# Sink attention and a feed-forward layer on one core: later splits moved one step up, one step's values pulled ahead, the last pair's products reordered

## The chip, the core and the metric

The kernel runs on one core of a Trainium2 chip, as one program without collectives. The metric is the time of one execution in device microseconds, taken as the median over runs. The parts of the core are called by the profile's names: PE (matmul) with PEld (its weight loads), ACT, DVE, POOL, and SP, which issues the DMAs.

## The reference, cut to what matters

```python
def _attn_ref(q, k, v, n_sink, window):            # (4, 8, 768, 64) each, n_sink 4, window 128
    scores = np.matmul(q, k.transpose(0, 1, 3, 2)) / np.sqrt(D)
    keep = is_sink | in_window                      # first n_sink keys, and 0 <= row - col < window
    scores = np.where(keep, scores, -1000000000.0)
    a = np.exp(scores - np.max(scores, axis=-1, keepdims=True))
    a = a / (np.sum(a, axis=-1, keepdims=True) + 1e-09)
    return np.matmul(a, v)

def _moe_ref(x, w_in, w_out):                       # x (3072, 512), w_in (512, 2048), w_out (2048, 512)
    h = x @ w_in
    sp = np.maximum(h, 0.0) + np.log1p(np.exp(-np.abs(h)))
    return (h * erf(sp)) @ w_out
```

The attention's result, with its eight heads side by side, is the x of the feed-forward layer.

## The kernel before

**Tiling.** The 3072 rows are twelve groups of 256 (`NG`), three to a batch. A group is four attention steps (`NPAIR`), one for each pair of heads, and then a feed-forward part. Step s belongs to group s // 4, so step 11 is the last of group 2, step 12 the first of group 3 and step 15 the last of group 3. All loops are unrolled in Python.

**An attention step.** `prep` transposes q and k (tile `tqk`, line 298) and ACT copies them (`kq`, line 301). `score` multiplies (line 349) into the single buffer `ps`. DVE masks (362) and finds the row's minimum (367). ACT takes the exponent (371); `mark["e", s]` names the last one. `norm` divides by the sums on DVE (378 to 386) and forms the sink part `snk` (390); `mark["s", s]` names it. `ptrans` transposes the weights on PE (`tp`, line 402, then `ts`, line 403; `mark["p", s]` is the last of `tp`), ACT copies them to `pa` and `pz` (409 to 415), POOL cuts them to the window (420). `av` multiplies by the values (457), and `xfin` splits the result into `xh` (ACT, 475) and `xl` (DVE, 476). `tqk`, `tp`, `ts` and `av` share two PSUM buffers.

**The feed-forward part.** For each of sixteen columns f of a group `hidden` multiplies (line 655, four chunks c of x, three products each) into one of two `h` buffers, two columns to a buffer. `act` runs on the pair: ACT lines 668 to 673, DVE 677, then `gh` (DVE 684) and `gl` (POOL 685). Its first product (677, out `u`, in `u` and `h`) is the last reader of the `h` buffer. `project` adds up both 128-row halves i of the group in two `o` tiles, three products each for every f (lines 700 to 702, the third with `gl`). `result` copies each `o` tile to `ot` (706), and line 617 writes it out. The tiles `u` of line 673 and `ot` share four buffers (`UB`).

**The splits.** Up to the middle of group 1 the weights are used as plain fp32. From then on each weight block is used as a rounded part and a rest: `wsplit` makes the first with an ACT cast (570) and the second with a DVE subtraction (571), in new tiles of the pool `wo` of 33 buffers. The eight splits n = 16 to 23, the first half of `w_out`, are due at m = 31 to 35 and have a mark of their own, `LATE`.

**What sets the order.** Each piece of work gets a priority key from the stage `a` in which it is written and a constant of its kind (`at`, `O`). A list scheduler then orders each engine's queue, taking in its own model of time the ready instruction of the smallest key. A split has a large key and is otherwise ready early, so it goes into the first free place. `follow(prev, ins)` adds an order without a semaphore: `ins` stands behind `prev` in the same engine's queue. Queues run in order on the chip.

**Step 11's exception.** In `core(s)`, from group 2 on, the values of step s - 2 are multiplied just ahead of the scores of step s, and the scores follow them. Step 11 alone is an exception: its `av` and `xfin` are written one and two stages behind the scores of step 12, and the scores of step 13 stand behind step 12's `tp` transposes instead.

Of the kernel before, what the change touches and what calls it, by code (L numbers as in the profile page):

```python
# [19 lines left out]
P = 128  # L20
# [19 lines left out]
NE, AL = 4, 2  # L40
# [3 lines left out]
LATE = 31  # L44

FH = 8

PW, EA = 256, 12
O = dict(prep=-100, norm=-100, core=-300, av=-300, load=-400, dup=-100, kcopy=-50, ptrans=-200, xfin=-100,
# [7 lines left out]
def kernel(  # L57
# [11 lines left out]
    nc = tc.nc  # L69
    B, H, S, D = q.shape  # L70
    NT, DM = out.shape
    DF = w_in.shape[1]
    NPAIR = H // 2
    NC = DM // P
    NF = DF // P
    GT = 256
    GPB = S // GT
    NG = B * GPB
# [56 lines left out]
    def fast_path():  # L135
        with ExitStack() as st:
# [145 lines left out]
            def follow(prev, ins):  # L282

                if prev is not None:
                    tc.add_manual_dep(
                        ins.ins, prev.ins.name,
                        mybir.DependencyInfo(mybir.DependencyClass.NoSync, mybir.DependencyReason.DATA), reason="order",
                    )
                return ins
# [15 lines left out]

            def core(s):

                prev = mark["p", s - 1] if s - AL == 3 * NPAIR - 1 else None
                late = s - AL >= 2 * NPAIR and s - AL != 3 * NPAIR - 1
                if late:  # L310
                    prev = av(s - AL)
                if s < NSTEP:
                    score(s, prev)
# [174 lines left out]
            for s in range(NSTEP + AL):  # L488
# [15 lines left out]
                if s < 2 * NPAIR:  # L504
                    x = pos(s) + (3 if s < NE else 5)
                    plan.setdefault(x, []).append(("av", av, s))
                    plan.setdefault(x + 1, []).append(("xfin", xfin, s))
                elif s == 3 * NPAIR - 1:
                    plan.setdefault(pos(s + 1) + 1, []).append(("av", av, s))
                    plan.setdefault(pos(s + 1) + 2, []).append(("xfin", xfin, s))  # L510
                if s - AL >= 2 * NPAIR and s - AL != 3 * NPAIR - 1:
                    plan.setdefault(pos(s) + 1, []).append(("xfin", xfin, s - AL))
            STAGES = ("xfin", "norm", "ptrans", "av", "kcopy", "prep", "core", "dup", "load")

# [48 lines left out]
            def wsplit(n, m):  # L563

                t = wf[n]
                d = wt[n] = wpool.tile([P, 2, DM], F32R, tag="wo", name=f"wt_{n}")
                x, y = mlp.mark[min((m - 1) // 2, NF) - 1]
                if m >= LATE:
                    x, y = mark["e", 3 * NPAIR], mark["s", 3 * NPAIR]
                follow(x, nc.scalar.copy(d[:, 0, :], t))  # L570
                follow(y, nc.vector.tensor_tensor(d[:, 1, :], t, d[:, 0, :].bitcast(F32), op=ALU.subtract))

# [24 lines left out]
            for m in range(-LEAD, NG * NF + LAG + 2):  # L597
# [11 lines left out]
                if 0 <= w < NG * NF:  # L609
                    g2, f2 = divmod(w, NF)  # L610
                    with at(a, "proj"):
                        mlp.project(gs[w // 2], g2, f2, lambda ins: follow(ahead if live and f and g >= 2 else None, ins))
                    if f2 == NF - 1:
                        for i in range(2):
                            r0 = (g2 * 2 + i) * P
                            with at(a, "res"):
                                nc.sync.dma_start(out[r0 : r0 + P, :], mlp.result(g2, i))
                if live:
                    if f == 0:
                        with at(a, "hid"):  # L620
# [17 lines left out]
    class make_mlp:  # L638
# [46 lines left out]
            nc.gpsimd.tensor_tensor(gl, acc, gh.bitcast(F32), op=ALU.subtract)  # L685
            return gh, gl

        def project(self, gt, g, f, behind=lambda ins: ins):
            if f == 0:
                for i in range(2):  # L690
                    self.acc[g, i] = self.ps_o.tile([P, DM], F32, tag="o", name=f"o_{g}_{i}")
            for i in range(2):
                o = self.acc[g, i]
                n0 = (f % 2) * GT + i * P
                ws = slice(n0, n0 + P)
# [5 lines left out]
                nc.tensor.matmul(o, gh[:, ws], wt[16 + f][:, 1, :], start=False, stop=False)  # L701
                nc.tensor.matmul(o, gl[:, ws], wt[16 + f][:, 0, :], start=False, stop=(f == NF - 1))  # L702

        def result(self, g, i):
            ot = self.work.tile([P, DM], F32, tag="u", bufs=UB, name=f"ot_{g}_{i}")
            nc.scalar.copy(ot, self.acc.pop((g, i)))  # L706
            return ot

    def general_path():
# [145 lines left out]
```

## Time and profile before

| what | value |
|---|---|
| time, median of 3 runs | 736.34 us (736.04 to 736.58) |
| the profiled execution | 736.62 us |
| its span, first to last instruction | 734.7 us |
| PE busy | 714.6 us, 97% |
| ACT busy | 552.2 us, 75% |
| DVE busy | 490.0 us, 67% |
| POOL busy | 215.8 us, 29% |
| granted TensorE clock, mean | 0.998 |

The profile is one execution. Its span leaves out 1.92 us of the 736.62 us that lie around the first and the last instruction. Times in its rows count from the first instruction. A row of the timeline gives start, length, engine, line, operation and tiles, the count where equal neighbours were merged, and in brackets the idle time of the engine just before it and what ended that. Matmuls are pipelined: the ends of two neighbours overlap, so distances are read from start to start.

### The profile page before, as it was taken

The page shows a single profiled execution, that of the slowest core. Times are in us where ns is not written, and L with a number is a line of the kernel's source. Part 1 is how long each engine was busy: PE and PEld are TensorE (multiplying, and loading weights), DVE is VectorE, ACT ScalarE, POOL GpSimd, SP SyncE. Part 2 cuts the span into 40 slices and gives each one's busy share as a digit, 9 for nine tenths or more (in the row PEclk, how much of TensorE's full clock was granted, in tenths as well). Part 3 has the DMA queues.
Part 4 walks back from the last instruction along what each step waited for, and adds up shares of the span by engine and source line. Part 5 has one row for each costly group of instructions (what it writes and reads, how often), then busy time and mean ns, then how long its engine had stood idle before and what let it go on. Part 6 is the DMA issues. An engine that isn't in the chain of part 4 may idle for free. (4 is left out here: it accounts for less than half of the span.)

```text
span 734.7 us, 16449 instructions
## 1 busy us (share of the span) xinstructions
PE 714.6 (97%) x5824; PEld 598.5 (81%) x5824; DVE 490.0 (67%) x1371; ACT 552.2 (75%) x1313; POOL 215.8 (29%) x306
## 2 busy tenths in 40 slices
PE   6889999999999999999999999999999999999997
PEld 3666667687888888888888888888888888898885
DVE  7999997877665765665665665665665666575352
ACT  5687759969887876976976885985986886776572
POOL 3411432042323322422323342233234223223221
PEclk9999999999999999999999999999999999999999
DMA  7999011113122121212222212311311321200000
GB/s 182 276 355 376 13 37 55 24 44 88 45 53 73 46 53 45 61 43 57 67 48 51 73 38 46 82 37 43 78 45 37 81 58 34 71 10 3 29 1 33
DMA packets 113001, 53.07 MB, mean 72 GB/s; under 512 B 91728, under 2 KB 105552, under 8 KB 112912
## 3 DMA queue, kind: packets, MB, share of 16 engines
q1 hardware_dynamic: 112352, 51.87, 26.2%
q8 instruction: 49, 0.80, 0.5%
q14 instruction: 40, 0.33, 0.1%
q10 hardware_dynamic: 560, 0.07, 0.1%
HBM read 38.01 MB, written 6.29 MB: 60 GB/s over the span
## 5 line engine op out<-in xcount | busy, mean ns | idle before, releaser
L655 PE MATMUL h<-xh,wt 128*128 128x256 f32 x1408 | 276.2, 284 | 0.7 <-DVE u L677 0.6
L655 PEld LDWEIGHTS h<-xh,wt 128*128 128x128 f32 x1408 | 223.8, 188 | 7.7 <-issue 1.8
L685 POOL TENSOR_TENSOR g<-u,g 128x512 fp32r<-128x512 f32 x84 | 111.2, 1324 | 366.4 <-DVE g L684 361.2
L655 PE MATMUL h<-xl,wt 128*128 128x256 f32 x704 | 197.9, 282 | 0.0
L673 ACT ACTIVATE u<-r 128x512 f32<-128x512 f32 x288 | 161.6, 622 | 14.9 <-DVE gf L677 4.9
L677 DVE SCALAR_TENSOR_TENSOR u<-u,u 128x512 f32<-128x512 f32 x168 | 131.9, 785 | 18.5 <-ACT u L673 4.0
L655 PEld LDWEIGHTS h<-xl,wt 128*128 128x128 f32 x704 | 132.1, 188 | 4.6 <-issue 0.7
L701 PE MATMUL o<-wt,g 128*128 128x512 f32 x336 | 133.9, 399 | 0.0
L700 PE MATMUL o<-wt,g 128*128 128x512 f32 x336 | 133.9, 398 | 0.0
L702 PE MATMUL o<-wt,g 128*128 128x512 f32 x336 | 130.0, 398 | 0.2 <-POOLq L823 0.2
L677 DVE SCALAR_TENSOR_TENSOR u<-u,h 128x512 f32<-128x512 f32 x84 | 57.6, 686 | 84.6 <-ACT u L673 82.5
L371 ACT ACTIVATE pst<-pst,neg 128x144 f32<-128x144 f32 x192 | 77.5, 406 | 26.6 <-DVE neg L367 25.7
L420 POOL TENSOR_SCALAR_AFFINE_SELECT pz<-pa 64x256 f32<-64x256 f32 (+1 forms) x96 | 54.2, 564 | 117.6 <-ACT pa L409 114.3
L700 PEld LDWEIGHTS o<-wt,g 128*128 128x128 f32 x336 | 63.0, 188 | 11.9 <-ACT ot L706 0.4
L702 PEld LDWEIGHTS o<-wt,g 128*128 128x128 f32 x336 | 61.9, 188 | 13.3 <-POOLq L823 0.7
L701 PEld LDWEIGHTS o<-wt,g 128*128 128x128 f32 x336 | 63.0, 188 | 11.3 <-issue 0.3
L668 ACT ACTIVATE r<-h 128x512 f32<-128x512 f32 x96 | 56.6, 589 | 17.8 <-PE h L655 14.3
L684 DVE CAST g<-u 128x512 fp32r<-128x512 f32 x84 | 36.6, 436 | 47.1 <-PE o L702 43.9
L670 ACT ACTIVATE r<-r 128x512 f32<-128x512 f32 x96 | 60.6, 632 | 2.5
L669 ACT ACTIVATE r<-r 128x512 f32<-128x512 f32 x96 | 60.7, 632 | 2.4
L301 ACT COPY kq<-tqk 128x512 f32<-128x512 f32 x48 | 27.8, 580 | 32.1 <-PE tqk L298 28.7
L349 PE MATMUL ps<-kq 64*64 64x208 f32 (+2 forms) x768 | 48.2, 361 | 0.6 <-ACT kq L304 0.5
(88 smaller groups left out, 923.1 us busy)
## 6 DMA issues: line engine op xcount, KB each, us to landing
ws<-in_moe_w_in_dram SPq DMA_DIRECT2D x16, 512.0 KB, 6.4
ws<-in_moe_w_out_dram SPq DMA_DIRECT2D x16, 512.0 KB, 8.3
out_dram<-ot SPq DMA_DIRECT2D x24, 256.0 KB, 2.2
v<-in_v_dram SPq DMA_DIRECT2D x56, 96.0 KB, 2.3
q<-in_q_dram SPq DMA_DIRECT2D x80, 64.0 KB, 2.1
k<-in_k_dram SPq DMA_DIRECT2D x80, 64.0 KB, 2.1
vz<-v SPq DMA_DIRECT2D x80, 64.0 KB, 2.0
kq<-kq SPq DMA_DIRECT2D x28, 64.0 KB, 2.1
```

The lines of the kernel that those rows point to most:

```text
L371: mark["e", s] = nc.scalar.activation(y, y, AF.Exp, bias=d["neg"][:, i, h : h + 1], scale=-1.0, accum_out=d["sum"][:, i, h : h + 1])
L420: nc.gpsimd.affine_select(out=out, in_=x, pattern=[[0, 2], [0, 2 - i0], [-sg, HP]], compare_op=op, fill=0.0, base=0, channel_multiplier=sg,)
L655: last = nc.tensor.matmul(o, wt[NC * j + c][:, p, fs], xt[e][:, c, :], start=(m == 0), stop=(m == len(ops) - 1))
L668: nc.scalar.activation(r, h, AF.Tanh, bias=b_t, scale=0.5)
L669: nc.scalar.activation(r, r, AF.Square, bias=b_v, scale=-0.5)
L670: nc.scalar.activation(r, r, AF.Square, bias=b_r)
L673: sq = nc.scalar.activation(u, r, AF.Square, bias=b_a[i], scale=CS)
L677: pr = nc.vector.scalar_tensor_tensor(out=acc, in0=u, scalar=CC[i] * CS**2, in1=x, op0=ALU.add, op1=ALU.mult)
L685: nc.gpsimd.tensor_tensor(gl, acc, gh.bitcast(F32), op=ALU.subtract)
L700: behind(nc.tensor.matmul(o, gh[:, ws], wt[16 + f][:, 0, :], start=(f == 0), stop=False))
L701: nc.tensor.matmul(o, gh[:, ws], wt[16 + f][:, 1, :], start=False, stop=False)
L702: nc.tensor.matmul(o, gl[:, ws], wt[16 + f][:, 0, :], start=False, stop=(f == NF - 1))
```

## The change

It has three parts.

- The exception of step 11 holds for steps 11 and 15. The values of step 15, until now multiplied ahead of the scores of step 17, are multiplied one stage behind the scores of step 16, and its `xfin` a stage later. The scores of step 17 stand behind step 16's `tp` transposes.
- The eight late splits stand behind step 11's last exponent on ACT and its `snk` on DVE, where they stood behind those of step 12.
- For the last two columns f of the last group, the six products of the first output tile are written ahead of the six of the second, where the order was column by column. The second tile's copy from PSUM is divided: ACT takes the left 256 columns and DVE the right 256.

```diff
+EARLY = (11, 15)
@@ core
-                prev = mark["p", s - 1] if s - AL == 3 * NPAIR - 1 else None
-                late = s - AL >= 2 * NPAIR and s - AL != 3 * NPAIR - 1
+                prev = mark["p", s - 1] if s - AL in EARLY else None
+                late = s - AL >= 2 * NPAIR and s - AL not in EARLY
@@ plan
-                elif s == 3 * NPAIR - 1:
+                elif s in EARLY:
                     plan.setdefault(pos(s + 1) + 1, []).append(("av", av, s))
                     plan.setdefault(pos(s + 1) + 2, []).append(("xfin", xfin, s))
-                if s - AL >= 2 * NPAIR and s - AL != 3 * NPAIR - 1:
+                if s - AL >= 2 * NPAIR and s - AL not in EARLY:
                     plan.setdefault(pos(s) + 1, []).append(("xfin", xfin, s - AL))
@@ wsplit
                 if m >= LATE:
-                    x, y = mark["e", 3 * NPAIR], mark["s", 3 * NPAIR]
+                    x, y = mark["e", 3 * NPAIR - 1], mark["s", 3 * NPAIR - 1]
@@ the loop over m
-                        mlp.project(gs[w // 2], g2, f2, lambda ins: follow(ahead if live and f and g >= 2 else None, ins))
+                        behind = lambda ins: follow(ahead if live and f and g >= 2 else None, ins)
+                        if w < NG * NF - 2:
+                            mlp.project(gs[w // 2], g2, f2, behind)
+                        elif f2 == NF - 1:
+                            for i in range(2):
+                                for e in range(2):
+                                    mlp.project(gs[w // 2], g2, f2 - 1 + e, behind, (i,))
@@
-                                nc.sync.dma_start(out[r0 : r0 + P, :], mlp.result(g2, i))
+                                nc.sync.dma_start(out[r0 : r0 + P, :], mlp.result(g2, i, NG - 1))
@@ project
-            for i in range(2):
+            for i in rows:
@@ result
-            nc.scalar.copy(ot, self.acc.pop((g, i)))
+            acc = self.acc.pop((g, i))
+            if g == last and i == 1:
+                nc.scalar.copy(ot[:, : DM // 2], acc[:, : DM // 2])
+                nc.vector.tensor_copy(ot[:, DM // 2 :], acc[:, DM // 2 :])
+            else:
+                nc.scalar.copy(ot, acc)
```

## Rows read from the trace of the kernel before

**Rows 1.** The page: busy time by engine, and PE's busy tenths in 40 slices.
```profile
PE 714.6 (97%) x5824; PEld 598.5 (81%) x5824; DVE 490.0 (67%) x1371; ACT 552.2 (75%) x1313; POOL 215.8 (29%) x306
...
PE   6889999999999999999999999999999999999997
```

**Rows 2.** Stretches of 10 us: length, busy PE, PEld, DVE, ACT, POOL, clock, DMA share, GB/s.
```profile
170.00:180.00 10.00, 9.41 (x67) 7.25 (x65) 8.79 (x23) 9.94 (x27) 2.45 (x5) 1.00 0.23 51
180.00:190.00 10.00, 9.69 (x89) 7.98 (x89) 6.05 (x21) 7.38 (x16) 3.26 (x7) 1.00 0.39 109
190.00:200.00 10.00, 9.68 (x78) 8.41 (x79) 7.00 (x15) 9.65 (x26) 4.28 (x6) 1.00 0.10 26
200.00:210.00 10.00, 10.00 (x87) 8.81 (x84) 7.59 (x25) 8.17 (x21) 1.49 (x2) 1.00 0.27 61
```

**Rows 3.** Timeline of PE: the work just behind its four waits.
```profile
176.59 0.39 PE L655 MATMUL h<-xh,wt 128*128 128x256 f32 x1 [0.59 <-DVE u L677]
...
179.76 0.40 PE L701 MATMUL o<-wt,g 128*128 128x512 f32 x1
180.29 0.50 PE L402 MATMUL tp<-ident,pst 128*128 128x128 f32 x2
...
186.38 0.44 PE L298 MATMUL tqk<-ident,k 128*128 128x128 f32 x2 [0.17 <-DMA v<-in_v_dram]
...
194.18 0.69 PE L402 MATMUL tp<-ident,pst 128*128 128x128 f32 x3 [0.32 <-ACT r L670]
```

**Rows 4.** Timeline of ACT and DVE: the late splits and what follows them.
```profile
166.91 2.69 ACT L570 CAST wt<-wf 128x512 fp32r<-128x512 f32 x5
...
174.06 1.67 ACT L673 ACTIVATE u<-r 128x512 f32<-128x512 f32 x3
...
168.45 4.30 DVE L571 TENSOR_TENSOR wt<-wf,wt 128x512 fp32r<-128x512 f32 x7
...
174.21 0.69 DVE L571 TENSOR_TENSOR wt<-wf,wt 128x512 fp32r<-128x512 f32 x1
...
175.85 0.69 DVE L677 SCALAR_TENSOR_TENSOR u<-u,h 128x512 f32<-128x512 f32 x1
```

**Rows 5.** Timeline of ACT, DVE and PE between step 11's and step 12's marks.
```profile
159.29 0.59 ACT L409 COPY pa<-tp 128x512 f32<-128x512 f32 x1 [1.37 <-PE tp L402]
...
162.59 0.37 ACT L475 CAST xh<-av 128x256 fp32r<-128x256 f32 x1 [2.07 <-PE av L457]
...
164.46 0.41 ACT L371 ACTIVATE pst<-pst,neg 128x144 f32<-128x144 f32 x1 [1.50 <-DVE neg L367]
...
162.99 0.43 DVE L476 TENSOR_TENSOR xl<-av,xh 128x256 fp32r<-128x256 f32 x1 [2.21 <-ACT xh L475]
...
165.26 0.42 DVE L476 TENSOR_TENSOR xl<-av,xh 128x256 fp32r<-128x256 f32 x1
...
165.75 0.37 PE L655 MATMUL h<-xl,wt 128*128 128x256 f32 x1
```

**Rows 6.** Timeline of SP and ACT: group 1's results on their way out.
```profile
180.89 1.06 SPq L617 DMA_DIRECT2D out_dram<-ot x2
...
185.06 0.64 ACT L673 ACTIVATE u<-r 128x512 f32<-128x512 f32 x1 [2.22 <-DMA out_dram<-ot]
185.60 0.73 ACT L413 COPY pz<-ts 64x256 f32<-64x256 f32 x2
```

**Rows 7.** Timeline of PE: step 13's scores, then step 17's behind step 15's values.
```profile
172.01 0.46 PE L349 MATMUL ps<-kq 64*64 64x144 f32 x2
172.40 0.33 PE L403 MATMUL ts<-ident,snk 128*128 128x128 f32 x1
172.66 0.85 PE L349 MATMUL ps<-kq 64*64 64x144 f32 x14
173.44 0.50 PE L701 MATMUL o<-wt,g 128*128 128x512 f32 x1
...
225.96 0.99 PE L349 MATMUL ps<-kq 64*64 64x208 f32 x16
226.88 0.44 PE L298 MATMUL tqk<-ident,k 128*128 128x128 f32 x2
```

**Rows 8.** The end: pieces of the last chain, and the output DMAs of the last stretch.
```profile
729.46 0.24 PE o L702
729.70 0.02 issue
729.73 0.58 ACT ot L706
...
DMA to landing us min/median/max: 2.2/2.5/2.7
```

More of the change, by code (lines that the diff above doesn't have):

```diff
@@ L686, in act, with project @@
             return gh, gl
-        def project(self, gt, g, f, behind=lambda ins: ins):
+        def project(self, gt, g, f, behind=lambda ins: ins, rows=(0, 1)):
             if f == 0:
@@ L702, in project, with result @@
                 nc.tensor.matmul(o, gl[:, ws], wt[16 + f][:, 0, :], start=False, stop=(f == NF - 1))
-        def result(self, g, i):
+        def result(self, g, i, last=None):
             ot = self.work.tile([P, DM], F32, tag="u", bufs=UB, name=f"ot_{g}_{i}")
-            nc.scalar.copy(ot, self.acc.pop((g, i)))
+            acc = self.acc.pop((g, i))
[4 more added lines that the diff above has]
+                nc.scalar.copy(ot, acc)
             return ot
```

## The prediction

> **What bounds the kernel now.** The page comes first: PE is busy 97% of the span, and its tenths read 9 or more from the fourth slice to the last but one [rows 1]. Work on the other engines therefore counts only where PE waits for it. Next I read the stretches of 10 us: behind 60 us PE falls short of full in few of them, and in the region that this change touches in three, from 170 to 200 us, while the next one is full again [rows 2]. The reader is to see there that ACT (9.94) and DVE (8.79) are nearly full in the first of these. Then the timeline of PE tells the four waits [rows 3]. They are 0.59 us in front of the hidden products at 176.59; a step from 179.76 to 180.29, 0.53 us where products of this kind follow each other at 0.23 (the pitch of the last chain's 0.24 in [rows 8]); 0.17 at 186.38 and 0.32 at 194.18. The idle column gives 0.59 + 0.17 + 0.32 and I add 0.30 for the second: about 1.4 us in all. That is the most that the first two parts can win by taking waits away. The third part is read from the last chain and the output's landing.
>
> **The splits: what they cost now.** The scheduler puts them as early as their mark lets it: five casts stand on ACT from 166.91, seven subtractions without a gap on DVE from 168.45, the eighth at 174.21 [rows 4]. They fall in front of the activation of the pair whose `h` buffer PE needs next. Line 673 starts at 174.06, and the first product on DVE, which frees the buffer, at 175.85; it ends at 176.54 and PE goes on at 176.59 [rows 3, 4]. So the first wait is the splits' doing. The second is the chain of step 13: its masks and minima stand behind the eighth subtraction, and its transposes come late. The third and the fourth are not theirs alone: ACT stands 2.22 us until an output DMA has landed, and the copies of `ts` that PE waits for (they end at 186.33) stand behind it in ACT's queue [rows 6]; the row's own releaser, a load, had long been done. The fourth is the normalising of step 14, whose DVE work queued behind the same stall.
>
> **The splits: where they go.** The work stays the same, eight casts and eight subtractions; no DMA and no PE instruction is moved with them. A cast takes 2.69 / 5 = 0.54 us and a subtraction 4.30 / 7 = 0.61 us [rows 4], so 4.3 us on ACT and 4.9 us on DVE. Behind step 11's marks ACT has idle times of 1.37 + 2.07 + 1.50 = 4.94 us and DVE of 2.21 us before step 12's softmax [rows 5]. ACT can hide all eight; DVE hides three or four, and the others come behind step 12's `snk` at the latest, where they used to be, but half of them and done some 2 us sooner. That is enough for the activation to be in time (its product at about 173 where PE needs it at 176). Queued behind a split are, on ACT, the copies of step 11's `tp` and the `xh` casts, on DVE the `xl` of steps 10 and 11. An instruction already running isn't cut short, so each idle time can overrun by one split. PE's hidden products at 165.75 start right behind the `xl` that ends at 165.68 [rows 5]: no slack there. I price this overrun between 0 and 0.6 us and take 0.2, since the idle times are wide against one split. Of the 1.4 us of waits I book all as won in the forecast: with the early backlog gone step 13's chain is ready sooner than PE, and `ts` is then transposed ahead of the stalled ACT instruction. Bounds: 0 (first rival) to 1.4.
>
> **Step 15's values.** Nothing is added; the value products, one cast and one subtraction move up some 10 us. A gain is excluded, because PE is full from 200 us on, at 9 or more tenths in every slice up to the end [rows 1, 2], and has no wait there that they could end. The cost is an extra change of PE's form of work. Step 13, which has this order now, shows it: its scores are cut by `ts` and take 172.01 to 173.44, 1.43 us, where step 17's take 225.96 to 226.88, 0.92 us, behind the values [rows 7]. The difference of 0.5 us holds about 0.1 us for `ts`, which is paid anyway. So 0 (scores that follow other work cleanly) to 0.5 us; I take 0.3. No load is late for it: the values' buffer comes free earlier, and SP's loads behind it with it. What becomes late next is nothing before step 17's own exponent, which gets more time.
>
> **The last pair.** All twelve products remain, and the third of a tile still waits for `gl`; while it waits, the second tile's two first products can fill in, as now. PE's end stays at 729.70. The first tile is complete some four products earlier than the second (4 x 0.24 = 0.9 us, now 0.7), so its copy and DMA leave about 0.25 us sooner. The second tile's copy now takes 0.58 us [rows 8]. Its halves: ACT's cast of 256 columns out of PSUM takes 0.37 us, DVE's subtraction with such an input 0.42 [rows 5], an upper bound for a plain copy. Side by side they take 0.42 us, 0.16 less; one behind the other 0.37 + 0.42 + 0.04 = 0.83, 0.25 more. The trace has no two engines reading one PSUM tile at once. The nearest rows, `xh` and `xl` of one `av` tile, run one after the other: 162.59 + 0.37 = 162.96, then 162.99 [rows 5], though there the second needs the first. I take the series. In return the two output DMAs are issued 1.1 us apart instead of 0.64. The last two landed after 2.2 and 2.7 us [rows 8]; if the second does as the first, 0 to 0.6 us come back, and I take 0.35. Sum of this part: 0.25 - 0.35 = -0.1, bounds +0.25 and -0.8. DVE's own closing instructions move behind its copy, under two microseconds of landing.
>
> The Trainium skill, "PSUM — Partial Sum Buffer", section "PSUM bank collisions raise a hardware error", says that two engines must not touch one bank and quadrant at the same time, reads against reads included, so that accesses have to be guarded by bank. The tile is one bank there; by that rule the halves go in series, the sum's choice, and the side-by-side case falls away. No run here shows such a collision.
>
> **The sum.** -1.4 + 0.2 + 0.3 - 0.1 = -1.0 us on the profiled execution: 736.62 - 1.0 = 735.6. The median of the runs is 0.28 below the profiled one, so 735.3.
>
> **Rivals.**
> 1. *The output DMA holds the gate.* Its issue at 180.89 follows a full SP queue of loads that this change doesn't move, and its landing at 185.05 doesn't care how early ACT is [rows 6]. If ACT's order stays, PE comes earlier to 186.38 and waits there for longer: the 0.59 and 0.30 won before are given back, and 0.17 and 0.32 stay. Then 0 + 0.2 + 0.3 - 0.1 = +0.4, with the overrun hidden behind the same gate +0.1 to +0.2: 736.7 profiled, 736.4 as median. For it: the wait is absolute in time. Against: it needs `ts` to stay behind line 673 in ACT's queue, and step 13's earlier chain speaks against that.
> 2. *More is won.* All waits go, the cut through step 13's scores goes too (0.4), step 15 costs nothing, the output comes 0.4 to 0.8 sooner: -1.4 - 0.4 - 0.5 = -2.3, 734.0 as median.
> 3. *Slower: the splits stand in front of step 11's `xl`.* If all eight subtractions are queued before 165.26, DVE needs 4.9 us where 2.21 us are free, and PE's products at 165.75 come 2.7 us late [rows 4, 5]. The later waits, which hang on ACT and DVE as well, aren't won back: +2.7 + 0.3 - 0.1 = +2.9, 739.2 as median. It decides from six subtractions ahead of that `xl` on (6 x 0.61 - 2.21 = 1.45 us).
> 4. *The splits don't move*, because no buffer of `wo` is free at step 11. The casts at 166.91 ran without a gap, so buffers were free then; whether earlier the rows don't show. +0.3 - 0.1: 736.5.
>
> **How the numbers follow.** What a measurement can tell from no change is 0.2%, 1.47 us: faster means below 734.87, slower above 737.81. Forecast 735.3, its own range 734.6 to 736.0: chance 0.45, of which 0.13 lies below 734.87. Rival 1: 0.25, same. Rival 2: 0.16, faster. Rival 3: 0.11, of which 0.10 is slower. Rival 4: 0.03, same. Faster 0.13 + 0.16 = 0.29; slower 0.10 and 0.02 for rival 1 with a long overrun, 0.12; same 0.59. The range leaves out half of rival 2 and nearly all of rival 3: 734.1 to 737.2.
>
> **What would show it.** Right: eight casts among ACT's idle times between 157 and 167, no more than four subtractions behind step 12's `snk`, no wait of PE at the product that frees the `h` buffer, PE full from 170 to 200. Wrong: an idle time of PE at the `xl` of step 11; ACT still standing for the output DMA and PE behind it; the scores of step 17 uncut at their old length; the two halves of the last copy overlapping, or the output landing no sooner.

## The result and the profile after

| kernel | median | range | ratio to before, 95% |
|---|---|---|---|
| before | 736.34 us | 736.04 to 737.9, 5 runs | |
| changed | 740.3 us | 740.01 to 740.98, 5 runs | 1.0053 (1.0041 to 1.0064) |

The change makes the kernel slower, by 4.0 us. The profiled execution took 740.3 us, its span 737.6 us, so 2.7 us lie outside the span, where the kernel before had 1.92. The page of after has PE as busy as [rows 1] and POOL busier, 223.5 us where it was 215.8, though POOL's work is the same:

```profile
PE 714.7 (97%) x5824; PEld 598.4 (81%) x5824; DVE 491.0 (67%) x1372; ACT 551.7 (75%) x1313; POOL 223.5 (30%) x306
```

The stretches of 10 us (columns as in [rows 2]) show where PE lost and won:

```profile
160.00:170.00 10.00, 8.01 (x105) 6.42 (x104) 8.81 (x22) 6.56 (x19) 7.90 (x8) 1.00 0.16 36
170.00:180.00 10.00, 10.00 (x84) 8.84 (x83) 5.68 (x22) 8.93 (x25) 2.59 (x5) 1.00 0.29 65
180.00:190.00 10.00, 10.00 (x94) 8.59 (x94) 3.86 (x11) 7.23 (x16) 2.71 (x5) 1.00 0.36 102
190.00:200.00 10.00, 10.00 (x64) 8.68 (x64) 7.75 (x26) 8.90 (x24) 1.63 (x3) 1.00 0.22 48
...
280.00:290.00 10.00, 9.27 (x94) 7.72 (x93) 5.48 (x28) 5.65 (x22) 3.89 (x6) 1.00 0.24 54
```

The three stretches from 170 to 200 us are full: the four waits of [rows 3] are gone, as forecast. In their place PE stands 2 us at 161 to 163 us, where it had been full, and again near 283 us. The timeline of PE names these places, and between them step 17's scores:

```profile
160.86 0.40 PE L708 MATMUL o<-wt,g 128*128 128x512 f32 x1
163.25 0.73 PE L709 MATMUL o<-wt,g 128*128 128x512 f32 x2 [1.99 <-POOL g L692]
...
228.51 0.56 PE L350 MATMUL ps<-kq 64*64 64x208 f32 x2
229.01 0.33 PE L404 MATMUL ts<-ident,snk 128*128 128x128 f32 x1
229.26 0.98 PE L350 MATMUL ps<-kq 64*64 64x208 f32 x14
230.18 0.38 PE L662 MATMUL h<-xl,wt 128*128 128x256 f32 x1
...
283.29 0.89 PE L403 MATMUL tp<-ident,pst 128*128 128x128 f32 x4 [0.25 <-DVE pst L387]
284.08 0.30 PE L404 MATMUL ts<-ident,snk 128*128 128x128 f32 x1
284.86 0.67 PE L458 MATMUL av<-pa,v 128*64 128x64 f32 x12 [0.47 <-ACT pa L410]
```

The first wait is the dearest, and its releaser is POOL. The product that stands is the third of the three (line 702 before, 709 after), the one with `gl`. The timeline of ACT, DVE and POOL tells why `gl` is late:

```profile
156.50 2.69 ACT L571 CAST wt<-wf 128x512 fp32r<-128x512 f32 x5
...
158.38 3.69 DVE L572 TENSOR_TENSOR wt<-wf,wt 128x512 fp32r<-128x512 f32 x6
...
158.54 4.65 POOL L692 TENSOR_TENSOR g<-u,g 128x512 fp32r<-128x512 f32 x1 [6.68 <-DVE g L691]
...
281.30 1.29 POOL L692 TENSOR_TENSOR g<-u,g 128x512 fp32r<-128x512 f32 x1 [0.36 <-DVE g L691]
...
281.91 0.70 DVE L379 TENSOR_SCALAR sum<-sum 128x4 f32<-128x4 f32 x1 [0.69 <-ACT pst L372]
```

Six late subtractions run on DVE from 158.38 to 162.07. POOL's one subtraction, 1.29 us at its usual length, starts at 158.54 and takes 4.65 us; it ends 1.12 us behind the last of the six. In the kernel before seven of the eight ran in a row at 168.45 [rows 4], when POOL had nothing to do. At 281.91 it is the other way round: a DVE operation on four columns takes 0.70 us, where its like took 0.17 at 156.63, and ends with POOL's subtraction at 282.6.

Last the end. The kernel ends with `tc.If(ok == 0)`, a second, general path that these executions jump over: each engine's program closes with a branch and, behind the jump, a semaphore instruction. The two halves of the last copy run in series, and these closing instructions follow (the view of the branch's line: count, duration in ns, start):

```profile
732.16 0.37 ACT L715 COPY ot<-o 128x256 f32<-128x256 f32 x1 [0.29 <-PE o L709]
...
732.56 0.42 DVE L716 COPY ot<-o 128x256 f32<-128x256 f32 x1 [4.06 <-ACT ot L715]
```
```profile
L835 DVEq COMPARE_BRANCH  x1: 72/72/72, 733.5 to 733.5; - x1
...
L835 ACTq EVENT_SEMAPHORE  x1: 17/17/17, 735.3 to 735.3; - x1
L835 DVEq EVENT_SEMAPHORE  x1: 21/21/21, 736.5 to 736.5; - x1
```

The same view of the kernel before, whose line is 823:

```profile
L823 DVEq COMPARE_BRANCH  x1: 72/72/72, 726.3 to 726.3; - x1
...
L823 DVEq EVENT_SEMAPHORE  x1: 21/21/21, 729.2 to 729.2; - x1
```

DVE needs 3 us from its branch to its next instruction. Before, these ran under the last products; after, they start only behind DVE's copy and end at 736.5, over a microsecond behind the output's landing at 735.2. Not every engine needs that long: POOL's step from the branch on takes 0.8 us (729.2 to 730.0).

**The balance of the two profiled executions.** From the first hidden product of group 1 (96.99 before, 97.94 after) to the last product PE took 632.70 and 634.18 us: +1.5. From the last product to the end of the execution: 5.0 + 1.94 and 5.44 + 2.74: +1.2. The first hidden product itself came 0.95 us later; up to there the programs are the same, and it lies between 96.6 and 99.3 us in all the runs below, so I don't count that part as the change's. By the medians it is 4.0 all the same, and by those of the runs below 2.6 for the first two parts and 1.2 for the third; where the traces' 2.7 and the medians' 4.0 part is not settled. Part of it may be the execution shown of the kernel before: three runs below that leave its middle as it is (`last`, `order`, `touch`) need 632.05 to 632.49 us for PE's stretch.

### The profile page after: what moved, and what is told of

Its sections match the earlier page's. It is cut to its first block, busy times and chain, and to the rows that moved or that the text cites. A ratio compares the mean times of both kernels' runs of the same rounds, so it can differ in the third digit from the quotient of the medians.

```text
span 737.6 us, 16453 instructions
## 1 busy us (share of the span) xinstructions
PE 714.7 (97%) x5824; PEld 598.4 (81%) x5824; DVE 491.0 (67%) x1372; ACT 551.7 (75%) x1313; POOL 223.5 (30%) x306
## 5 line engine op out<-in xcount | busy, mean ns | idle before, releaser
L692 POOL TENSOR_TENSOR g<-u,g 128x512 fp32r<-128x512 f32 x84 | 114.9, 1368 | 360.0 <-DVE g L691 343.5
L421 POOL TENSOR_SCALAR_AFFINE_SELECT pz<-pa 64x256 f32<-64x256 f32 (+1 forms) x96 | 57.2, 596 | 120.5 <-ACT pa L410 117.2
```

The lines of the kernel that those rows point to most:

```text
L421: nc.gpsimd.affine_select(out=out, in_=x, pattern=[[0, 2], [0, 2 - i0], [-sg, HP]], compare_op=op, fill=0.0, base=0, channel_multiplier=sg,)
```

## The experiments

Five theories are named in the expectations. **A**: VectorE's row of subtractions holds up GpSimd's, and TensorE waits for that. **B**: the prediction's own account. **C**: the end costs because VectorE's closing instructions come behind its share of the copy. **D**: the waits further down come from how much of TensorE's work stands in its queue between a step's last score product and its first transposition (the cover of the softmax), and behind `tp`, until the next product needs one of the two PSUM buffers that `tqk`, `tp`, `ts` and `av` share. The cover is counted in the queue's order by the pitches of the rows, 0.118 us for `h`, 0.233 for `o`, 0.109 for `tqk`; step 16 has 21 + 21 + 4 products before, 7.8 us. **E**: step 15's cost is an output transfer stuck behind loads.

| run | what differs from before | ratio, 95% |
|---|---|---|
| splits | the splits behind step 11 | 1.0027 (1.0015 to 1.0039) |
| step15 | step 15's values | 1.0024 (1.0014 to 1.0034) |
| step15b | the same again | 1.0028 (1.0017 to 1.0039) |
| last | the third part | 1.0019 (1.0009 to 1.0028) |
| order | the third part without the divided copy | 1.0003 (0.9994 to 1.0013) |
| touch | 16 columns of the last copy on DVE | 1.0020 (1.0010 to 1.0029) |
| splits15 | parts one and two | 1.0035 (1.0022 to 1.0048) |
| casts | only the eight casts behind step 11 | 1.0061 (1.0039 to 1.0082) |
| sq15_pr15 | the splits behind pair 15's own instructions | 1.0050 (1.0033 to 1.0067) |
| first19 | the first three splits behind step 11 | 0.9981 (0.9971 to 0.9990) |
| first19b | the same again | 0.9976 (0.9967 to 0.9986) |
| first20 | the first four | 1.0028 (1.0018 to 1.0038) |
| fill16 | first19, nine products moved | 0.9999 (0.9989 to 1.0010) |
| step15_pool | step15, two outputs issued by POOL | 1.0013 (1.0004 to 1.0022) |

**Each part alone.** `splits` and `step15` have one of these two edits each; `last` has the whole third part of the change's diff, `order` the same without its last hunk and the argument that goes with it (the copy stays whole on ACT).

```diff
@@ splits
-                    x, y = mark["e", 3 * NPAIR], mark["s", 3 * NPAIR]
+                    x, y = mark["e", 3 * NPAIR - 1], mark["s", 3 * NPAIR - 1]
@@ step15, and the same two tests in the plan
-                prev = mark["p", s - 1] if s - AL == 3 * NPAIR - 1 else None
-                late = s - AL >= 2 * NPAIR and s - AL != 3 * NPAIR - 1
+                prev = mark["p", s - 1] if s - AL in (11, 15) else None
+                late = s - AL >= 2 * NPAIR and s - AL not in (11, 15)
```

> The kernel before with the late splits' mark moved to step 11 and nothing else. Theory A, from the changed kernel's trace: six subtractions in a row on DVE keep POOL from its own two-input subtraction, which takes 4 to 5 us instead of 1.3, and PE waits about 2 us for that rest near 161 us; the four waits of before between 170 and 200 us (1.4 us) are mostly gone. So +0.3 to +1.2 us, with that one wait of about 2 us in the trace. Theory B, from the prediction: the splits hide, the 1.4 us are won and the loss comes from the other parts: -0.8 to -1.4 us and no wait of PE near 161 us.

> The kernel before with step 15's values ahead and nothing else. The prediction's term: +0.3 us (0 to 0.5), as an extra change of PE's form of work, with step 17's scores cut by a transpose. Rival: the reordering that it sets off further on costs more, as two waits of together 1 us in front of a transpose and of values near 282 us in the changed kernel: +1.0 to +1.6 us. If these two waits belong to the splits instead, none of them is seen here.

> The kernel before with the last pair's order and the divided copy, and nothing else. The prediction's term: -0.1 us (+0.25 to -0.8). Theory C, from the changed kernel's trace: the copy's halves run in series, the output lands no later, but DVE now passes the branch at the program's end 3 us after the last copy and the closing barrier waits for it: +0.4 us inside the span and +0.8 us behind it, +1.2 us in all.

> The kernel before with the last pair's products first tile then second, and ACT copying both tiles whole. Theory C: DVE has no work behind the products, so the end keeps its length or wins from the first tile's earlier output: -0.1 to -0.5 us. If the order of the products itself costs, as a longer wait for the last rest, +0.4 us or more.

All three parts cost: 738.55 us, 738.42 us and 738.01 us, beside 736.78 of before. The order of the last products alone costs nothing, 736.72. So the divided copy is what costs at the end, 1.2 to 1.3 us, and theory B falls for every part. Where the end's cost shows was expected otherwise: in `last` the span behind the last product grows by 2.0 us (7.03 for 5.00) and what lies outside it shrinks by 0.5 (1.39 for 1.94), while in the changed kernel both grow; only the sums agree, and how they divide isn't explained. The two waits of the whole change near 283 us are in neither `splits` nor `step15`: they belong to both parts together. In the run of the splits PE (timeline) waits at the same product as in the whole change, and twice more at step 16:

```profile
162.20 0.73 PE L702 MATMUL o<-wt,g 128*128 128x512 f32 x2 [1.99 <-POOL g L685]
...
225.21 0.89 PE L402 MATMUL tp<-ident,pst 128*128 128x128 f32 x4 [0.66 <-DVE pst L386]
...
226.77 0.55 PE L457 MATMUL av<-pa,v 128*64 128x128 f32 x8 [0.47 <-ACT pa L409]
```

At 207 us, counted by the pitches of the products done since 140 us, this run stands within 0.2 us of the kernel before: the 2 us at 162 are paid for by before's four waits and the loss around them. What stays is step 16: another 1.8 us, so that the run costs more than the 0.3 to 1.2 us expected.

**The end: 16 columns.**

```diff
-            nc.scalar.copy(ot, self.acc.pop((g, i)))
+            acc = self.acc.pop((g, i))
+            if g == last and i == 1:
+                nc.scalar.copy(ot[:, : DM - 16], acc[:, : DM - 16])
+                nc.vector.tensor_copy(ot[:, DM - 16 :], acc[:, DM - 16 :])
+            else:
+                nc.scalar.copy(ot, acc)
```

> The kernel before with one edit: of the very last tile's copy, ScalarE moves 496 columns and VectorE the other 16; the order of the last products and everything else stay. Theory C (VectorE's program ends with a branch and a fetch of instructions that took it 3 us in the kernel before under the last products, and in the changed kernel came behind its copy): the two engines' parts take about as long in series as ScalarE's whole copy did (0.58 us there, so 0.6 to 0.9 here), but VectorE's last instructions again come 3 us behind its copy, and the time rises by 1.0 to 1.4 us, to 1.0014 to 1.0019 of before, with the span's end about 7.0 us behind the last product instead of 5.0, or the difference outside the span. Rival (the cost of the divided copy lies in the copy and in the transfer behind it): the copy ends at most 0.3 us later, and the time is 0 to 0.3 us over before, 1.0000 to 1.0004.

It was 737.8 beside 736.38, so +1.4 us, with the copy only 0.19 us longer (0.81 behind the last product, before 0.62) and the landing no later (3.20 behind it, before 3.39). DVE (timeline, then the branch's line) closes 3 us behind its branch, which follows its 16 columns:

```profile
729.35 0.17 DVE L709 COPY ot<-o 128x16 f32<-128x16 f32 x1 [4.26 <-ACT ot L708]
```
```profile
L828 DVEq COMPARE_BRANCH  x1: 72/72/72, 730.3 to 730.3; - x1
...
L828 DVEq EVENT_SEMAPHORE  x1: 21/21/21, 733.3 to 733.3; - x1
```

Theory C holds. The price was about the same for 256 columns (1.2 us) and for 16 (1.4): what counts is that DVE is last.

**Parts one and two together.** Both edits of the diff above.

> The whole change without its third part: the splits behind step 11 and step 15's values moved, the end as in before. Theory C (the end's cost of 1.2 to 1.3 us comes from VectorE's share of the last copy and stands apart from all the rest): 1.0 to 1.4 us under the changed kernel, so 2.3 to 2.9 us over before, 1.0031 to 1.0040; TensorE's instructions are the changed kernel's but for their order at the end, with its waits near 161 us (2 us), 282 and 284 us (0.4 and 0.75 us). Rival (the three costs share a wait downstream, and the end takes over what the middle gives back): 3.2 us or more over before, 1.0043 or more.

739.15 beside 736.53: 2.6 us, and 1.15 under the changed kernel, as C says. PE's waits are the changed kernel's: 1.99 at 162.76 for POOL, 0.25 at 283.44 and 0.47 at 285.00. The two parts cost 2.6 where alone they cost 1.8 and 1.6: they are not independent, for the second part moves the thin cover from step 16 (4.2 us in `splits`, 6.9 here) to step 20 (7.0 here, 8.3 before), where `av` again stands right behind `ts`. Counted by the pitches of the products done, this run is within 0.2 us of the kernel before at 207 us, about 0.6 behind it between 240 and 280 us, and about 1.7 from 300 us on (an estimate): the larger part of the loss falls at step 20. No run changes step 20 alone, so that it is the cover there that costs is read from the trace and not tested.

**Casts without subtractions.**

```diff
-                    x, y = mark["e", 3 * NPAIR], mark["s", 3 * NPAIR]
+                    x, y = mark["e", 3 * NPAIR - 1], mark["s", 3 * NPAIR]
```

> Only the eight casts on ScalarE go behind step 11; the eight subtractions on VectorE stay behind step 12's snk, where GpSimd was idle in before. Theory A: without subtractions near 160 us GpSimd's g - gh takes 1.2 to 1.5 us, and TensorE has no wait over 0.4 us at 158 to 163 us. Theory D: TensorE's queue then holds only 1.1 us of work between step 16's last score product and its first transposition (7.8 in before, 4.2 with casts and subtractions moved), so it waits 3 to 5 us in front of step 16's transpositions near 220 us, and 0.5 to 0.8 us more in front of the values' product that stands directly behind ts. Both: 1.5 to 4 us over before, 1.0020 to 1.0055, by waits in another place than with all splits moved. Rival of A (the casts cost, not the subtractions): the wait of 2 us near 161 us stays. Rival of D (the scheduler's other choices outweigh the distance): no wait over 1 us at step 16, and the time within 1 us of before.

Timeline of POOL and PE:

```profile
158.27 1.30 POOL L685 TENSOR_TENSOR g<-u,g 128x512 fp32r<-128x512 f32 x1 [6.65 <-DVE g L684]
...
225.94 0.89 PE L402 MATMUL tp<-ident,pst 128*128 128x128 f32 x4 [2.62 <-DVE pst L386]
...
227.60 0.55 PE L457 MATMUL av<-pa,v 128*64 128x128 f32 x8 [0.57 <-ACT pa L409]
```

Both hold. Without subtractions POOL takes its 1.30 us and PE doesn't wait near 160; the cast is innocent there. And with a cover of 1.1 us (6 `h` and 4 `tqk`) PE waits 2.62 us at step 16, less than the 3 to 5 expected, and 0.57 behind it. The time, +4.3 us, is a little over what was expected, and not by the waits alone. Right behind them, in the execution shown (740.87 us, at the median), from 228.3 to 231.7 us, PE was granted half its clock, 1.2 GHz for 2.4 (stretch of 2 us, columns as in [rows 2], the clock is the number 0.50):

```profile
229.00:231.00 2.00, 2.00 (x19) 1.18 (x15) 0.86 (x3) 0.19 (x1) 0.38 (x1) 0.50 0.43 93
```

The products of these 3.4 us are worth 1.6 us at the usual pitches, so the fall cost about 1.8 us (an estimate). The profiles of before and of the whole change have none between 29 and 734 us.

**Subtractions later, same queue of PE.**

```diff
-                    x, y = mark["e", 3 * NPAIR], mark["s", 3 * NPAIR]
+                    x, y = mlp.mark[15][0], mlp.mark[15][1]
```

> The run of the splits alone, with the five to seven late copies and subtractions behind pair 15's own last square (ScalarE) and last product (VectorE) instead of behind step 11's exponentials and xl. TensorE's queue is the same as in that run. Theory A (the row of subtractions on VectorE held up GpSimd's subtraction g - gh, 1.28 us in before and 4.65 us in the changed kernel, and by it the product o that waited 1.99 us at 160 us): with the subtractions behind that pair's third product they no longer run beside GpSimd's earlier operation, or fewer do, so GpSimd's longest g - gh near 157 to 165 us is under 2.5 us and TensorE's wait of 2 us on it is gone or under 0.7 us. Theory D (the two waits near 224 to 226 us in front of step 16's transpositions and product by the values come from how much of TensorE's work stands in its queue between that step's last score product and its first transposition, 4.2 us here and in that run against 7.8 in before): those waits stay, 1.2 to 1.9 us together. With both the time is 0.0 to 1.4 us over before, 1.0000 to 1.0019. Rival of A (the wait at 160 us is ScalarE's and VectorE's own lateness by the overrun of copies): the wait of 1.5 to 2 us stays in some form on the same products. Rival of D (the waits near 225 us are what the wait at 160 us left behind): they shrink under 0.5 us, and the time is 1 us or more under before.

Timeline of POOL and PE:

```profile
158.01 1.30 POOL L685 TENSOR_TENSOR g<-u,g 128x512 fp32r<-128x512 f32 x1 [6.69 <-DVE g L684]
...
165.15 0.51 PE L655 MATMUL h<-xh,wt 128*128 128x256 f32 x2 [1.13 <-ACT xh L475]
166.06 0.79 PE L457 MATMUL av<-pa,v 128*64 128x128 f32 x8 [0.40 <-POOL pa L420]
```

POOL is free again at 158 us (A; its next subtraction, beside the moved row, takes 1.69), and the two waits at step 16 are there to within a hundredth, 0.65 and 0.47 (D). But the time, +3.7 us, is far over the 0 to 1.4 expected: the casts and subtractions now stand in front of step 11's `xh`, of POOL's cut and of `xl`, and PE waits 1.13, 0.40 and 0.24 us there. That is the path of the prediction's third rival. Here too the granted clock fell behind the first two of these waits, from 166.2 to 169.6 us, over products worth 1.6 us, so again about 1.8 us (an estimate) are the clock's and not the waits':

```profile
167.00:169.00 2.00, 2.00 (x21) 1.88 (x18) 1.90 (x8) 0.78 (x3) 0.20 (x1) 0.50 0.34 74
```

**How many splits.** Only the first three, then the first four of the eight, go behind step 11 (`n < 19` and `n < 20`):

```diff
-                    x, y = mark["e", 3 * NPAIR], mark["s", 3 * NPAIR]
+                    x, y = (mark["e", 11], mark["s", 11]) if n < 19 else (mark["e", 12], mark["s", 12])
```

> Only the splits of weight pieces 16 to 18 go behind step 11; those of 19 and on stay behind step 12 as in before. Theory A: at most three subtractions in a row on VectorE hold GpSimd's g - gh up by less than 2 us more, so TensorE's wait on it near 160 us is under 0.7 us. Theory D: the work in TensorE's queue between a step's last score product and its first transposition is 6.0 us for step 16 and 7 or more for steps 12 to 15, near what before has, so there is no wait over 0.4 us near 224 to 226 us. Of before's four waits between 176 and 195 us one or two are still there. Time 0.3 to 1.5 us under before, 0.9980 to 0.9996. Rival (the place of the splits doesn't matter by number, any split behind step 11 costs): 0.5 us or more over before.

> One more split than in the run of pieces 16 to 18: those of 16 to 19 go behind step 11, the others behind step 12. TensorE's queue then holds 2.6 us of work between step 12's last score product and its first transposition (7.1 in before), and 8.2 for step 16. Theory D: a softmax chain of about 5 us isn't covered by that, so TensorE waits 2 to 3 us in front of step 12's transpositions or the values' product behind them, near 170 to 185 us, and no wait over 0.4 us near 224 to 226 us; the time is 0.5 us or more over the run of pieces 16 to 18. Rival (what counts is the load on VectorE and GpSimd near 160 us alone): one split more or less moves the time by less than 0.5 us between these two runs, and there is no wait over 1 us in front of step 12's transpositions.

> The run of pieces 16 to 18 once more, beside the run with the nine products moved. Theory D: 0.9 to 1.6 us under before (0.9978 to 0.9988), with the wait of 0.5 to 0.6 us in front of step 15's product by the values, near 223 us. Rival (what was measured before was chance): within 0.5 us of before.

Three splits are faster than before: 735.06 beside 736.38, and 735.02 beside 736.53 in the repeat, 1.3 and 1.5 us. It is the fastest kernel of this study. Timeline of DVE, POOL and PE in the repeat:

```profile
157.87 1.89 DVE L571 TENSOR_TENSOR wt<-wf,wt 128x512 fp32r<-128x512 f32 x3
...
158.03 2.88 POOL L685 TENSOR_TENSOR g<-u,g 128x512 fp32r<-128x512 f32 x1 [6.67 <-DVE g L684]
...
160.96 0.73 PE L702 MATMUL o<-wt,g 128*128 128x512 f32 x2 [0.21 <-POOL g L685]
...
223.59 0.55 PE L457 MATMUL av<-pa,v 128*64 128x128 f32 x8 [0.57 <-ACT pa L409]
```

None of before's four waits is left in it, where one or two were expected, though five of the eight splits still stand behind step 12. D was wrong on one point: it expected no wait over 0.4 us near 224, and the one in front of `av` is there, 0.57 us. Its cover is enough for the transpositions (6.0 us), but `av` stands right behind `ts`, with 0.03 us of work between, and waits until ACT has copied `tp` out of the shared buffer.

Four splits lose it all, 738.55 beside 736.38. In the timeline of POOL and PE:

```profile
157.18 3.47 POOL L685 TENSOR_TENSOR g<-u,g 128x512 fp32r<-128x512 f32 x1 [6.67 <-DVE g L684]
...
160.70 0.73 PE L702 MATMUL o<-wt,g 128*128 128x512 f32 x2 [0.80 <-POOL g L685]
...
168.57 0.66 PE L402 MATMUL tp<-ident,pst 128*128 128x128 f32 x4 [1.11 <-ACT kq L304]
```

Step 16 is clean, as expected, and step 12 isn't. The wait in front of its transpositions is 1.11 us, not 2 to 3, and what ends it is a copy of `kq` that stands behind two casts on ACT and holds the shared buffer: the place was foreseen, the releaser not. The execution shown is the fastest of its nine (737.4 us; PE's stretch is 633.69 for 632.70 before), so of the 2.2 us that the median loses the trace shows about half.

**Nine products moved.** In the kernel of `first19` the first nine products of one hidden column are put behind step 16's transpositions:

```diff
-                            ahead = mlp.hidden(hp, xp[g], f)
+                            ahead = mlp.hidden(hp, xp[g], f, lambda ins: follow(mark["p", 16] if m == 50 else None, ins))
@@ hidden
...
+                if m == 0:
+                    behind(last)
```

> The run of pieces 16 to 18, and in it one thing of TensorE's queue: the first nine products of the hidden column f = 2 of group 3, which stood ahead of the o products there, stand behind step 16's four transpositions. Theory D, second half (the wait of 0.57 us, 0.81 us of lost pitch, at 223.51 in that run comes from step 15's product by the values standing directly behind ts: it takes the buffer which tp holds until ScalarE has copied it): nine products of 0.118 us cover the copy, the wait is gone or under 0.2 us, and the time is 0.4 to 0.8 us under the run of pieces 16 to 18. The work between step 16's last score product and its first transposition sinks from 6.0 to 5.0 us by this; where 4.2 us left a wait of 0.66 us, 5.0 leaves none over 0.2 us. Rival (ScalarE is late there whatever TensorE does in the meantime, and the wait moves with it): a wait of 0.5 us or more stays in front of the values' product or appears in front of the transpositions, and the time is that of the run of pieces 16 to 18 within 0.3 us.

It was 736.54, 1.5 us over `first19b` in the same comparison: a miss. The wait in front of `av` is gone (0.57 to 0.00 us), as D says, but a larger one came in front of the transpositions. Timeline of DVE, POOL and PE:

```profile
222.56 0.43 DVE L686 CAST g<-u 128x512 fp32r<-128x512 f32 x1
...
223.11 1.89 DVE L386 TENSOR_SCALAR pst<-pst,sum 128x128 f32<-128x128 f32 x4
...
223.07 1.26 POOL L687 TENSOR_TENSOR g<-u,g 128x512 fp32r<-128x512 f32 x1 [4.51 <-DVE sum L379]
...
224.56 1.03 PE L402 MATMUL tp<-ident,pst 128*128 128x128 f32 x4 [1.69 <-DVE pst L386]
```

The scheduler also moved one DVE instruction, the cast of `gh`, from behind step 16's normalising to the front of it (in `first19b` it runs at 222.43, behind). That sets POOL's subtraction free just as DVE starts to normalise, and the four operations take 1.89 us instead of 0.88 in `first19b` (221.44, with POOL idle). In this execution the granted clock fell as well, from 225.1 to 228.5 us, right behind the wait:

```profile
226.00:228.00 2.00, 2.00 (x13) 1.69 (x13) 0.00 (x0) 0.45 (x2) 1.52 (x4) 0.50 0.03 8
```

It is the slowest of the eleven, 739.52 us. The fastest, 735.35, had a mean granted clock of 1.000 and so no fall; for the others the record doesn't tell. So how the 1.5 us of the medians divide between the wait and the clock is open.

The cover that a step needs has no fixed length: scores to transpositions took 3.8 us in `casts` (1.1 of cover and 2.6 of wait), 4.8 in `splits`, 6.7 here and 7.2 at step 20 of the changed kernel, by what else stands on DVE and whether POOL runs beside it. D stands as a statement of where the waits fall, not of their size.

**Step 15 and the output.** With step 15's values alone the copies of group 2's outputs come 5.6 and 6.3 us later than before (240.2 and 241.9 in the repeat, for 234.7 and 235.7; the first trace, 740.84 us and the slowest of its nine, had lost over 2 us before group 1 already), since the products that fill `o` were put later, and their DMAs then fall among the loads of q and k in SP's queue.

```diff
-                                nc.sync.dma_start(out[r0 : r0 + P, :], mlp.result(g2, i))
+                                (nc.gpsimd if g2 == 2 else nc.sync).dma_start(out[r0 : r0 + P, :], mlp.result(g2, i))
```

> The run of step 15's values alone, with one thing changed: the two output transfers of group 2 are issued by GpSimd instead of SyncE, where they stood among the loads of q and k in SyncE's queue (issued at 245.52 and 247.06, though the first copy ended at 243.25). The orders of TensorE, ScalarE and VectorE are the same as in that run. Theory E (ScalarE's u stood 1.66 us at 248.03 until that output had landed, which made TensorE wait at 249 to 251 us): the output lands by 246 us, ScalarE's wait falls under 0.4 us, TensorE's two waits (0.51 and 0.15 us idle, 1.0 us of lost pitch) go, and the time is 0.8 to 1.6 us under that of step 15's values alone, so within 0.8 us of before (0.9998 to 1.0011). Rival (the cost is in the order of TensorE's products themselves, the values' product and the scores at other places): at most 0.4 us is won and the time stays 1.2 us or more over before, 1.0016 or more.

> Step 15's values alone once more, beside the run whose group 2 outputs GpSimd issues. Both theories: 1.2 to 2.0 us over before (1.0016 to 1.0027), with ScalarE's u standing 1 us or more for the output near 248 us and TensorE's waits behind it. If what was seen before was one disturbed execution, the time is within 0.8 us of before, and the wait isn't there.

Timeline of ACT and SP in the repeat of `step15`, then of ACT and POOL with the outputs on POOL:

```profile
240.24 0.59 ACT L706 COPY ot<-o 128x512 f32<-128x512 f32 x1 [0.35 <-PE o L702]
...
245.16 0.63 ACT L673 ACTIVATE u<-r 128x512 f32<-128x512 f32 x1 [1.21 <-DMA out_dram<-ot]
...
242.82 0.42 SPq L617 DMA_DIRECT2D out_dram<-ot  x1
```
```profile
244.24 0.63 ACT L673 ACTIVATE u<-r 128x512 f32<-128x512 f32 x1 [0.16 <-DMA out_dram<-ot]
...
241.27 0.71 POOL L617 DMA_DIRECT2D out_dram<-ot  x1 [4.29 <-ACT ot L706]
```

ACT's stand falls from 1.21 to 0.16 us, PE's products from 244 to 250 us take 1.0 us less, its whole stretch 1.3 us less (632.45 for 633.72), and the time falls from 738.12 to 737.03. Theory E holds for 1.1 of the 1.9 us of this part alone. In the whole change it has no share: there the copies come 1.1 us later than before (235.79 and 236.79), both outputs are issued in a row (timeline of SP), and ACT doesn't stand for them.

```profile
236.41 1.36 SPq L624 DMA_DIRECT2D out_dram<-ot  x2
```

Of the part alone, the other 0.8 (1.0013, interval 1.0004 to 1.0022) stays: PE's own stretch is no longer than before's (632.45 and 632.70), 0.4 us lie behind the last product (5.43 + 1.93 for 5.0 + 1.94), which may be the price of a DMA queue more, and the start was 0.5 us later. What of it belongs to step 15's order wasn't settled.

## Why the prediction was wrong, step by step

Predicted were 735.3 us (734.1 to 737.2); measured 740.3. Every term of the sum failed on its own, and no rival had the measured time.

- **The splits, -1.4 and +0.2.** That all four waits go was right; the rows of after show it. The step that failed is "queued behind a split": it named ACT's and DVE's instructions and left out POOL, who is on another queue and yet waits. The overrun measured 2.0 us at the first place, for the 0.2 booked (bounds 0 to 0.6), so that this region nets nothing. The count of hidden splits was wrong too: I let DVE hide three or four and put the rest behind step 12; six ran in one row, and all eight ahead of step 12's masks. Rival 3 had six subtractions as its point of decision and 739.2 as its time, near to the 738.55 of the splits alone, but by another path: not `xl` was late, but `gl`. Its path was seen in `sq15_pr15`.
- **What is late next.** The prediction took the order of PE as given. A moved mark lets the scheduler order PE's products anew for tens of microseconds, and the cover of step 16 shrank from 7.8 to 4.2 us. That is the 1.8 us which the run of the splits keeps. In the whole change step 16 has its cover back and step 20 is short of it, with waits of 0.25 and 0.47 us; the larger part of PE's net loss of 1.5 us falls there. No step of the prediction looked at either place.
- **Step 15's values, +0.3 (0 to 0.5).** Alone they cost 1.6 to 1.9. The cut through the scores that the term was made of didn't appear alone (0.92 us, as in before); in the whole change it did and was larger than its bound: step 17's scores go from 228.51 to 230.18, 1.67 us for 0.92 in [rows 7]. Alone, the larger part was rival 1's mechanism at another output: an output was late, behind the loads, and the prediction had looked only at loads ("no load is late for it"). The rival was priced only at 185 us [rows 6], where it didn't decide. In the whole change that output isn't late, and by the pitches counted for `splits15` the part's price is in the cut scores and at step 20.
- **The last pair, -0.1 (+0.25 to -0.8).** The copy in series was right: 0.37 + 0.42, its end 0.24 us later than before for the 0.25 booked. So was that the output lands somewhat sooner after the last product (3.09 for 3.39 us). Wrong was "under two microseconds of landing" for DVE's closing instructions. They take 3 us from the branch on and so outlast the landing; the tail grew by 1.2 us. The trace of before has that duration (726.3 to 729.2), and no row of the prediction held it.
- **The range.** The chances let only 0.12 fall on slower, because each part's loss was bounded by the engines named in its own rows. They were of one sign and added up: 2.6 us for the first two parts and 1.2 for the third.

The Trainium skill, "PSUM — Partial Sum Buffer", section "PSUM bank collisions raise a hardware error", which the prediction set beside the choice of the series, wants the accesses of two engines to one bank guarded. The trace of after agrees in so far as the halves don't overlap: ACT's ends at 732.53 and releases DVE's at 732.56; no run shows a collision. The late `gl` is told by the Trainium skill too, "SBUF — State Buffer", section "SBUF: two separate sides": VectorE and GpSimd share a pair of ports as an exclusive lock, a VectorE operation with two SBUF inputs against a GpSimd one that reads SBUF, and the loser waits in full. The traces agree: POOL's end stands 1.12 to 1.15 us behind the last subtraction, be there three, four or six, so that POOL waited for the whole row and not for one instruction of it.

## What to carry to other kernels

Before moving work into idle time of an engine, look at who runs beside it, not only at who queues behind it: here DVE's idle time was POOL's busy time. Where a scheduler orders the queues, compare the bound engine's whole order before and after, and count the work between a product's last input and its first use; and check what an engine still has to do at its program's end before giving it the last word.

## What the runs showed of the hardware

- POOL's 128x512 subtraction takes 1.28 to 1.30 us by itself, 2.88 beside three DVE subtractions in a row, 3.47 beside four and 4.65 beside six. Whatever their number, 1.12 to 1.15 us of it remain behind the last: it got next to nothing done beside or between them.
- It holds DVE as well: four 128x128 operations with one tensor input 1.89 for 0.88 us, one of four columns 0.70 for 0.17.
- From its branch at the end of the program, over the general path, DVE takes 2.9 to 3.0 us to its next instruction (726.3 to 729.2, 733.5 to 736.5, 730.3 to 733.3), ACT 2.6 to 2.9 and POOL 0.7 to 0.8. Before, DVE had no work in the last products, and its 3 us ran under them.
- The granted clock of PE fell from 1.0 to 0.5 (2.4 to 1.2 GHz) for 3.4 us right behind waits in three profiled executions: 1.13 and 0.40 us in `sq15_pr15`, 2.62 and 0.57 in `casts`, 1.69 in `fill16`. The wait of 1.99 us in the changed kernel, `splits` and `splits15` was followed by none. Each fall cost about 1.8 us, as estimated above for the first two.
